# Retention before a feed-forward block: one product of 192 columns for a piece's outputs and its new state

## The chip, the cores and the metric

The kernel runs on one core of a Trainium2 chip. The metric is the device time of one execution in microseconds, a median of several; differences of 0.2% and more can be told from no change. The core has a matrix engine (TensorE, PE in the profile; its weight loads stand apart as PEld), a vector engine (VectorE, DVE), a scalar engine (ScalarE, ACT), a general engine (GpSimd, POOL) and a sync engine (SyncE, SP) that issues nearly all transfers. TensorE writes to PSUM, a small memory of banks of 128 partitions x 512 floats[...].

## The reference

All data are fp32. 8 batches, 8 heads, 576 tokens, 64 columns a head; then 4608 tokens of 512 columns through a feed-forward block of 2048.

```python
scores = scale * np.matmul(q, k.transpose(0, 1, 3, 2))
gamma = 1.0 - 2.0 ** (-5.0 - np.arange(H, dtype=np.float32))
Dmat = np.where(rel >= 0, gamma[:, None, None] ** rel[None, :, :], 0.0)
attn = np.matmul(scores * Dmat[None, :, :, :], v)
x = attn.transpose(0, 2, 1, 3).reshape(B * S, H * D)
h = x @ w_in
sp = np.maximum(h, 0.0) + np.log1p(np.exp(-np.abs(h)))
out = (h * erf(sp)) @ w_out
```

The weights come as float64 and are rounded to fp32 in the kernel. Because the decay is a power of the distance, a batch can be worked through in pieces with a state: a piece's output is its own masked scores times values, plus its queries times the sum of keys x values of all earlier pieces, decayed.

## The kernel before

**Pieces.** A batch of 576 tokens is four pieces of 128 and a rest of 64; the rests of two batches make one piece. That is 36 pieces, numbered from 0 here and in the code; 8, 17, 26 and 35 are the short ones, and 0, 4, 9, 13, 18, 22, 27 and 31 begin a batch and have no earlier state. Each piece has three stages. `transposes` (L315) brings queries and keys into columns: for early pieces on TensorE with ScalarE copying out, later from squares of 32x32 loaded by DMA and turned by VectorE (`STREAM_TRANSPOSE`, L326). `scores` (L341) makes eight products, two heads at a time on the two halves of the array's rows, and VectorE masks them into `sT`. `outputs` (L354) makes, in this order on TensorE,

- eight products values x scores (L365), 128 rows, 64 columns of the array, 128 columns streamed;
- where there is an earlier state, eight products state x queries (L376), 64 rows and 64 columns of the array each;
- for a piece of 128 tokens, eight products values/keys (L388), 64 columns streamed, giving keys x values of this piece (`kv`).

Heads come in four pairs p of two, e; the output of head e of pair p goes to the half (e + p) % 2 of the partitions, so the state products of two pairs lie on four different quarters of the array. Then VectorE scales the outputs into `x` (`scaled`, L400), adds `kv` to the earlier state (L421) and GpSimd multiplies by the decay of 128 tokens (L427; VectorE where the batch begins). The result, `kept[b]`, is the state that the next piece's L376 reads.

**Order.** The stages stand in one list (L434-439): transposes of i + 1, outputs of i, scores of i + 1, and so on. `attend` runs the next of them between two products of the feed-forward block, so on TensorE a stage is followed by a group of eight matrix records ("product") of that block, which is worked in chunks of 512 tokens with a Strassen-like scheme of seven products (`First` for w_in, `Second` for w_out). ScalarE copies the accumulators out (t<-a, o<-a), takes softplus and erf with a table load each; all engines work through their instructions in the order of the program. GpSimd weighs values by the decay (`weigh_values`, L306) before they are used and does part of the weights' rounding.

**Loads.** Rows of keys and values of piece i + 3 are asked for at the end of `outputs(i)` (L430), queries and squares of piece i + 2 in `transposes(i)` (L339), all on SyncE's queue. Rows of keys have four buffers of their own. At the start, `keep_busy` (L735) multiplies a tile of ones while nothing has landed.

Of the kernel before, what the change touches and what calls it, by code (L numbers as in the profile page):

```python
# [18 lines left out]
P = 128  # L19
B, H, S, D = 8, 8, 576, 64  # L20
D_MODEL, D_FF = 512, 2048
NP = H // 2
# [9 lines left out]
def decays():  # L32

    gamma = 1.0 - 2.0 ** (-5.0 - np.arange(H, dtype=np.float64))
    pairs = gamma.reshape(2, NP)
    row = pairs.repeat(D, axis=0)
    out = np.where(np.arange(NP) % 2 == 0, row, np.roll(row, D, axis=0))  # L40
    t = np.arange(P)
    parts = []
    for n in (P, D):
        j = t % n
        i = np.arange(n).reshape(-1, n // 32).T.reshape(-1)
        gk = pairs.T.reshape(1, H) ** -j[:, None]
        gq = out[:, :, None] ** i[None, None, :] / math.sqrt(D)
        i_all = np.concatenate([i + a for a in range(0, P, n)])
        tri = (i_all[None, :] >= t[:, None]) & (i_all[None, :] // n == t[:, None] // n)
        parts += [gk, gq, row**P, tri] if n == P else [gk, gq, tri]  # L50
    return np.concatenate([x.reshape(P, -1) for x in parts], axis=1).astype(np.float32)
# [3 lines left out]
def kernel(  # L55
# [66 lines left out]

    def load_squares(i, name, src):
# [12 lines left out]
    def load_rows(i, name, src, bufs):  # L136
        if name == "q":
            t = raw.tile([P, NP, P * D // SQ], FP32, tag="qs", name="raw_q", bufs=bufs)
            t = t.rearrange("p a x -> p (a x)")[:, : H * D].rearrange("p (h d) -> p h d", h=H)
        else:  # L140
# [23 lines left out]
    ones = cpool.tile([P, P], FP32, name="ones")  # L164
    nc.vector.memset(ones, 1.0)
# [26 lines left out]
    def parts():  # L192

        w2 = w_in.rearrange("(e c d) (h f) -> c e d h f", c=n_dc, d=D, h=2)
        for g in range(n_g):
            for dc in range(n_dc):
                a = A11 if dc < 2 else A12
                src = [(heads[(e + dc) % 2], w2[dc, e, :, :, 2 * g * GW : 2 * (g + 1) * GW]) for e in range(2)]
# [104 lines left out]
    kept = {}  # L303
    weighed = set()

# [9 lines left out]
    def transposes(i):  # L315
        t = live[i] = loaded.pop(i)
        if i < SQUARES:
            weigh_values(i)
# [22 lines left out]
    def scores(i):  # L341
        t = live[i]
        sT = t["sT"] = att.tile([P, 2, NP, P], FP32, tag="sT", name="sT")
# [10 lines left out]
    def outputs(i):  # L354
        segments = pieces[i]
        t = live.pop(i)
# [3 lines left out]

        b, s0, n, _ = segments[0]
        o = [ps_at.tile([P, NP, P], FP32, tag="at", name=f"o{j}") for j in range(2)]
        for p in range(NP):
            for e in range(2):
                nc.tensor.matmul(  # L365
                    o[p % 2][heads[(e + p) % 2], p // 2, :],
                    lhsT=t["v"][:, 2 * p + e, :],
                    rhs=t["sT"][:, e, p, :],
# [4 lines left out]
        for state, r0, m in seen:  # L373
            for p in range(NP):
                for e in range(2):
                    nc.tensor.matmul(  # L376
                        o[p % 2][heads[(e + p) % 2], p // 2, r0 : r0 + m],
                        lhsT=state[heads[e], p, :],
                        rhs=t["qT"][heads[e], p, r0 : r0 + m],
# [4 lines left out]
        if n == P:  # L384
            kv = flat(o[0])[:, 2 * P :].rearrange("p (a d) -> p a d", a=NP)
# [14 lines left out]
        def scaled(j):  # L400
            to = x[0, c][:, j:NP:2, at : at + P]
            if c < n_ch - 1:
                by = (gq if n == P else gq2)[:, j::2, :].unsqueeze(2).to_broadcast([P, 2, P // n, n])
                dst, got = (y.rearrange("p a (m i) -> p a m i", i=n) for y in (to, o[j][:, :2]))
# [3 lines left out]
            for r0 in range(0, P, n):  # L408
# [3 lines left out]
                    for y in (o[j][:, :2, r0 : r0 + n], (gq if n == P else gq2)[:, j::2, :])  # L412
# [4 lines left out]
        if n == P:  # L417
            sums = kv
            if s0 > 0:
                sums = att.tile([P, NP, D], FP32, tag="sums", name="sums")  # L420
                tt(sums, kv, kept[b], ALU.add)  # L421

            if b % 2 == 0 and s0 + P + D == S:
                new = att.tile([P, NP, D], FP32, tag="last", name="last", bufs=1)
            else:
                new = att.tile([P, NP, D], FP32, tag="state", name="state")
# [3 lines left out]
        load(i + 3, "kv")  # L430
# [304 lines left out]
    def keep_busy(n):  # L735
        for _ in range(n):
            nc.tensor.matmul(idle[:, :P], lhsT=ones, rhs=ones, start=True, stop=True)
# [126 lines left out]
```

## Time and profile before

| | |
|---|---|
| time, median of 3 | 1027.68 us (1027.46 to 1027.72) |
| span of the profiled execution | 1024.0 us |
| TensorE busy | 1017.6 us, 99% |
| VectorE, ScalarE, GpSimd busy | 667.6, 390.2, 122.6 us |
| records of L365, L376, L388 | 576, 512, 512; 41.1, 19.5, 21.5 us busy |
| pieces run until | some 314 us |

A fp32 product stands as two records in the profile. Busy time of a group on TensorE is the union of overlapping records, so what a group costs is better read from starts: the start of the next group minus its own. "128*64 128x64" is rows*columns of the array, then partitions x elements streamed. In a group line the figures behind the bar are busy time and mean duration; what stands after the second bar is idle time of the engine just before and what ended it. In the list in order of time the first column is the start, the second the length, and a bracket gives idle time before and what ended it.

### The profile page before, as it was taken

The numbers are of one execution on the slowest core, as the hardware profiler recorded it, in microseconds if no ns is written. First come the engines' busy times: TensorE is split into PE (matmuls) and PEld (weight loads), VectorE is DVE, ScalarE is ACT, GpSimd is POOL, SyncE is SP. The second block draws the span as 40 slices with busy tenths as digits, with TensorE's granted clock in tenths as the row PEclk, the third lists the DMA queues.
The fourth block names the chain that finished last, engine by engine and source line by source line (L and its number), as shares of the span: only waits on it lengthen the run. The fifth ranks groups of instructions, "written<-read, shape, count | busy, mean of one in ns | idle before, by whom it ended". The sixth has DMA issues, their size and how long they took to land.

```text
span 1024.0 us, 15958 instructions
## 1 busy us (share of the span) xinstructions
PE 1017.6 (99%) x6348; PEld 876.0 (86%) x6348; DVE 667.6 (65%) x1062; ACT 390.2 (38%) x481; POOL 122.6 (12%) x122
## 2 busy tenths in 40 slices
PE   9999999999999999999999999999999999999998
PEld 8787888888888888888888888888888888888887
DVE  3769777976976656656666666666567655555555
ACT  3354134234134444334343444444433333333332
POOL 2143112122312110010001001000100000000000
PEclk9999999999999999999999999999999999999999
DMA  9998989979974354544444345444433333444434
GB/s 200 203 242 175 232 203 223 255 150 253 244 195 150 106 161 145 165 160 154 164 147 158 124 147 162 165 144 144 144 124 124 124 131 127 131 136 131 126 88 119
DMA packets 146986, 165.76 MB, mean 162 GB/s; under 512 B 97376, under 2 KB 121568, under 8 KB 138848
## 3 DMA queue, kind: packets, MB, share of 16 engines
q1 hardware_dynamic: 144832, 163.57, 56.4%
q10 hardware_dynamic: 2080, 1.18, 0.5%
q8 instruction: 50, 0.82, 0.4%
q14 instruction: 24, 0.20, 0.1%
HBM read 117.52 MB, written 47.19 MB: 161 GB/s over the span
## 4 chain that ended last, share of the span: by engine, by line
PE 94%; DMA 3%; DVE 2%; SPq 1%; POOL 1%; issue 0%; ACTq 0%; DVEq 0%; POOLq 0%
PE a L604 24%; PE a L496 23%; PE g L604 12%; PE g L496 12%; PE e L496 6%; PE e L604 6%; PE o L365 3%; PE s L347 3%; PE o L388 2%; DMA raw_k<-in_k_dram 1%; PE o L376 1%; DMA raw_v<-in_v_dram 1%; PE f L668 1%; SPq L147 1%; PE p L550 1%; PE h L668 1%
## 5 line engine op out<-in xcount | busy, mean ns | idle before, releaser
L496 PE MATMUL a<-x,wa 128*128 128x256 f32 x1088 | 258.3, 380 | 0.0
L496 PEld LDWEIGHTS a<-x,wa 128*128 128x128 f32 x1088 | 205.7, 190 | 28.5
L604 PE MATMUL a<-wb,s 128*128 128x256 f32 x840 | 200.0, 381 | 0.0
L604 PEld LDWEIGHTS a<-wb,s 128*128 128x128 f32 x840 | 158.4, 190 | 22.9 <-ACT o L618 0.7
L99 DVE TENSOR_TENSOR t<-g,t 128x512 f32<-128x512 f32 x68 | 47.0, 691 | 151.9 <-ACT t L526 114.1
L496 PE MATMUL g<-x,wa 128*128 128x256 f32 x544 | 129.2, 380 | 0.0
L496 PEld LDWEIGHTS g<-x,wa 128*128 128x128 f32 x544 | 102.8, 190 | 14.4
L99 DVE TENSOR_TENSOR o<-a,o 128x512 f32<-128x512 f32 x104 | 71.4, 687 | 46.4 <-PE a L604 46.4
L521 ACT COPY t<-a 128x512 f32<-128x512 f32 x34 | 19.9, 586 | 188.3 <-PE a L496 188.3
L99 DVE TENSOR_TENSOR t<-t,s 128x1024 f32<-128x1024 f32 x72 | 88.4, 1267 | 0.0
L274 POOL TENSOR_TENSOR wraw<-wraw 128x512 f32<-128x512 f32 x28 | 29.4, 1051 | 438.1 <-DVE wraw L272 184.4
L565 ACT ACTIVATE s<-t 128x1024 f32<-128x1024 f32 x72 | 72.1, 1049 | 24.6 <-DVE t L99 24.5
L99 DVE TENSOR_TENSOR x<-x 128x512 f32<-128x512 f32 x115 | 75.8, 693 | 1.2
L532 ACT COPY t<-a 128x512 f32<-128x512 f32 x34 | 19.9, 586 | 144.4 <-PE a L496 144.4
L569 ACT ACTIVATE s<-s 128x1024 f32<-128x1024 f32 x72 | 72.1, 1049 | 0.4
L604 PE MATMUL g<-wb,s 128*128 128x256 f32 x280 | 66.7, 381 | 0.0
L604 PE MATMUL e<-wb,t 128*128 128x256 f32 x280 | 66.6, 380 | 0.0
L604 PE MATMUL a<-wb,t 128*128 128x256 f32 x280 | 66.6, 380 | 0.0
L604 PE MATMUL g<-wb,t 128*128 128x256 f32 x280 | 66.4, 380 | 0.0
L99 DVE TENSOR_TENSOR sT<-s,cst 128x512 f32<-128x512 f32 x72 | 46.2, 682 | 30.4 <-PE s L347 30.4
L496 PE MATMUL e<-x,wa 128*128 128x256 f32 x272 | 64.8, 381 | 0.0
L99 DVE TENSOR_TENSOR o<-g,o 128x512 f32<-128x512 f32 x70 | 47.9, 684 | 20.9 <-ACT o L618 18.1
(86 smaller groups left out, 1247.1 us busy)
## 6 DMA issues: line engine op xcount, KB each, us to landing
od<-o SPq DMA_DIRECT2D x54, 512.0 KB, 3.3
x<-xd SPq DMA_DIRECT2D x27, 1024.0 KB, 4.8
o<-od SPq DMA_DIRECT2D x27, 1024.0 KB, 5.4
raw_qs<-in_q_dram SPq DMA_DIRECT2D x96, 112.0 KB, 4.4
raw_ks<-in_k_dram SPq DMA_DIRECT2D x84, 112.0 KB, 4.2
xd<-x SPq DMA_DIRECT2D x9, 1024.0 KB, 5.2
raw_v<-in_v_dram SPq DMA_DIRECT2D x64, 128.0 KB, 4.5
wraw<-in_moe_w_in_dram SPq DMA_DIRECT2D x32, 256.0 KB, 5.7
```

The lines of the kernel that those rows point to most:

```text
L99: nc.vector.tensor_tensor(out=out, in0=in0, in1=in1, op=op)
L274: engine.tensor_tensor(out=r_f, in0=high_f, in1=r_f, op=ALU.mult)
L347: nc.tensor.matmul(ps[e][:, p, :], lhsT=t["kT"][heads[e], p, :], rhs=t["qT"][heads[e], p, :], start=True, stop=True)
L365: nc.tensor.matmul(o[p % 2][heads[(e + p) % 2], p // 2, :], lhsT=t["v"][:, 2 * p + e, :], rhs=t["sT"][:, e, p, :], start=(p < 2), stop=(no ...
L388: nc.tensor.matmul(kv[heads[e], p, :], lhsT=t["k"][:, 2 * p + e, :], rhs=t["v"][:, 2 * p + e, :], start=False, stop=(p == NP - 1), skip_gr ...
L496: nc.tensor.matmul(acc[:, j * TH : (j + 1) * TH], lhsT=weights["wa", self.g][:, a, d, j * P : (j + 1) * P], rhs=x[self.g, self.c][a][:, d, :],
L521: nc.scalar.copy(out=self.t1[:, 1], in_=self.a)
L532: nc.scalar.copy(out=self.t2[:, 0], in_=self.a)
L565: nc.scalar.activation(self.s[:, j], t, AF.Softplus)
L569: nc.scalar.activation(self.s[:, j], self.s[:, j], AF.Erf)
L604: nc.tensor.matmul(acc[:, tp, :], lhsT=left[:, j * TH + tp * P : j * TH + (tp + 1) * P], rhs=weights["wb", self.g][:, b, j, :], start=(sta ...
L668: nc.tensor.matmul(acc, lhsT=left[:, j * TH + tp * P : j * TH + (tp + 1) * P], rhs=weights["wb", self.g][:, b, j, :], start=(b in (B11, B2 ...
```

## The change

From piece 13 on, the rows of keys stand right beside a head's masked scores in one tile, 128 + 64 columns a head. Values x [scores | keys] is then one product of 192 columns: it gives the outputs and, in the last 64 columns, (keys x values) transposed. VectorE turns that in blocks of 32x32 (`STREAM_TRANSPOSE`), GpSimd adds the earlier state and multiplies by the decay, once into `new` (kept in the turned-block form for the next sum) and once into `whole`, a tile of 128x128 for a pair with one head's 64x64 state in each diagonal quarter and zeros elsewhere. ScalarE then moves the off-diagonal blocks of 32 to their places (`place_state`, four copies), called at the start of the next `transposes` or `outputs` stage. The state product for a piece of 128 tokens becomes four products with the full array. For this each head's output must lie in the half e of the partitions for every pair, in all pieces. Keys' rows, `sT` of early pieces and the new combined slots (three) share one tile `keys`; from piece 13 on rows of keys are loaded two pieces ahead in place of three. `whole`, zero at first, also takes the place of the ones in `keep_busy`.

```diff
--- before.py
+++ after.py
@@ -37,14 +37,13 @@
     gamma = 1.0 - 2.0 ** (-5.0 - np.arange(H, dtype=np.float64))
     pairs = gamma.reshape(2, NP)
     row = pairs.repeat(D, axis=0)
-    out = np.where(np.arange(NP) % 2 == 0, row, np.roll(row, D, axis=0))
     t = np.arange(P)
     parts = []
     for n in (P, D):
         j = t % n
         i = np.arange(n).reshape(-1, n // 32).T.reshape(-1)
         gk = pairs.T.reshape(1, H) ** -j[:, None]
-        gq = out[:, :, None] ** i[None, None, :] / math.sqrt(D)
+        gq = row[:, :, None] ** i[None, None, :] / math.sqrt(D)
         i_all = np.concatenate([i + a for a in range(0, P, n)])
         tri = (i_all[None, :] >= t[:, None]) & (i_all[None, :] // n == t[:, None] // n)
         parts += [gk, gq, row**P, tri] if n == P else [gk, gq, tri]
@@ -120,6 +119,29 @@
     SQUARES_K = 3 * PC
     SQ = 32
 
+    BESIDE = 13
+    WIDE = P + D
+
+    keys = att.tile([P, 3, H * WIDE], FP32, name="keys", bufs=1)
+
+    def beside(i):
+
+        return keys[:, i % 3, :].rearrange("p (h x) -> p h x", h=H)
+
+    def rows_of_keys(i):
+        if i < BESIDE:
+            at = i % 4 * H * D
+            return keys.rearrange("p a x -> p (a x)")[:, at : at + H * D].rearrange("p (h d) -> p h d", h=H)
+        return beside(i)[:, :, P:]
+
+    def scores_of(i):
+        if i < BESIDE:
+            at = (4 * D + i % 2 * P) * H
+            return keys.rearrange("p a x -> p (a x)")[:, at : at + H * P].rearrange(
+                "p (e a j) -> p e a j", e=2, a=NP
+            )
+        return beside(i)[:, :, :P].rearrange("p (a e) j -> p e a j", e=2)
+
     def load_squares(i, name, src):
         t = raw.tile([P, NP, P * D // SQ], FP32, tag=name + "s", name=f"raw_{name}s", bufs=2)
         for b, s0, n, r0 in pieces[i]:
@@ -137,6 +159,8 @@
         if name == "q":
             t = raw.tile([P, NP, P * D // SQ], FP32, tag="qs", name="raw_q", bufs=bufs)
             t = t.rearrange("p a x -> p (a x)")[:, : H * D].rearrange("p (h d) -> p h d", h=H)
+        elif name == "k":
+            t = rows_of_keys(i)
         else:
             t = raw.tile([P, H, D], FP32, tag=name, name=f"raw_{name}", bufs=bufs)
         for b, s0, n, r0 in pieces[i]:
@@ -161,8 +185,9 @@
                 elif name == "v" or i < SQUARES_K or len(pieces[i]) == 1:
                     t[name] = load_rows(i, name, src, 4)
 
-    ones = cpool.tile([P, P], FP32, name="ones")
-    nc.vector.memset(ones, 1.0)
+
+    whole = cpool.tile([P, NP, P], FP32, name="whole")
+    nc.vector.memset(whole, 0.0)
     load(0)
     cst = cpool.tile([P, CONST_COLS], FP32, name="cst")
     nc.sync.dma_start(out=cst[:, :CONST_FIRST], in_=consts[:, :CONST_FIRST])
@@ -195,7 +220,7 @@
         for g in range(n_g):
             for dc in range(n_dc):
                 a = A11 if dc < 2 else A12
-                src = [(heads[(e + dc) % 2], w2[dc, e, :, :, 2 * g * GW : 2 * (g + 1) * GW]) for e in range(2)]
+                src = [(heads[e], w2[dc, e, :, :, 2 * g * GW : 2 * (g + 1) * GW]) for e in range(2)]
 
                 yield src, "wa", g, a, dc % 2, ["wa"] if g > 0 and dc == n_dc - 1 else []
             for f in range(2):
@@ -301,7 +326,21 @@
         return xpool.tile([P, n_dc + 3, TCH], FP32, tag="x", name="x")
 
     kept = {}
+    squares_kept = [None]
+    unplaced = []
     weighed = set()
+
+    def place_state():
+
+        while unplaced:
+            dst, src = unplaced.pop()
+            for e in range(2):
+                for a in range(2):
+                    rows, to = (slice(e * D + x * SQ, e * D + (x + 1) * SQ) for x in (a, 1 - a))
+                    cols = (e * D if dst is whole else 0) + a * SQ
+                    nc.scalar.copy(
+                        out=dst[to, :, cols : cols + SQ], in_=src[rows, :, (1 - a) * SQ : (2 - a) * SQ]
+                    )
 
     def weigh_values(i):
 
@@ -314,6 +353,7 @@
 
     def transposes(i):
         t = live[i] = loaded.pop(i)
+        place_state()
         if i < SQUARES:
             weigh_values(i)
         for name in "qk":
@@ -340,7 +380,7 @@
 
     def scores(i):
         t = live[i]
-        sT = t["sT"] = att.tile([P, 2, NP, P], FP32, tag="sT", name="sT")
+        sT = t["sT"] = scores_of(i)
         ps = [ps_at.tile([P, NP, P], FP32, tag="at", name=f"s{e}") for e in range(2)]
         for p in range(NP):
             for e in range(2):
@@ -353,36 +393,45 @@
 
     def outputs(i):
         segments = pieces[i]
+        place_state()
         t = live.pop(i)
         seen = [(kept[b], r0, n) for b, s0, n, r0 in segments if s0 > 0]
 
 
-
         b, s0, n, _ = segments[0]
+        wide = n == P and i >= BESIDE
         o = [ps_at.tile([P, NP, P], FP32, tag="at", name=f"o{j}") for j in range(2)]
+        kv = flat(o[0])[:, 2 * P :].rearrange("p (a d) -> p a d", a=NP)
+        o = [flat(y).rearrange("p (a x) -> p a x", a=2) if wide else y[:, :2] for y in o]
         for p in range(NP):
             for e in range(2):
+                h = 2 * p + e
                 nc.tensor.matmul(
-                    o[p % 2][heads[(e + p) % 2], p // 2, :],
-                    lhsT=t["v"][:, 2 * p + e, :],
-                    rhs=t["sT"][:, e, p, :],
+                    o[p % 2][heads[e], p // 2, : WIDE if wide else P],
+                    lhsT=t["v"][:, h, :],
+                    rhs=beside(i)[:, h, :] if wide else t["sT"][:, e, p, :],
                     start=(p < 2),
                     stop=(not seen and p >= NP - 2),
                     skip_group_check=True,
                 )
         for state, r0, m in seen:
             for p in range(NP):
+                dst, by = o[p % 2][:, p // 2, r0 : r0 + m], t["qT"][:, p, r0 : r0 + m]
+                if state is whole and n == P:
+                    nc.tensor.matmul(
+                        dst, lhsT=whole[:, p, :], rhs=by, start=False, stop=(p >= NP - 2), skip_group_check=True
+                    )
+                    continue
                 for e in range(2):
                     nc.tensor.matmul(
-                        o[p % 2][heads[(e + p) % 2], p // 2, r0 : r0 + m],
-                        lhsT=state[heads[e], p, :],
-                        rhs=t["qT"][heads[e], p, r0 : r0 + m],
+                        dst[heads[e]],
+                        lhsT=state[heads[e], p, heads[e] if state is whole else slice(0, D)],
+                        rhs=by[heads[e]],
                         start=False,
                         stop=(p >= NP - 2),
                         skip_group_check=True,
                     )
-        if n == P:
-            kv = flat(o[0])[:, 2 * P :].rearrange("p (a d) -> p a d", a=NP)
+        if n == P and not wide:
             for p in range(NP):
                 for e in range(2):
                     nc.tensor.matmul(
@@ -401,7 +450,7 @@
             to = x[0, c][:, j:NP:2, at : at + P]
             if c < n_ch - 1:
                 by = (gq if n == P else gq2)[:, j::2, :].unsqueeze(2).to_broadcast([P, 2, P // n, n])
-                dst, got = (y.rearrange("p a (m i) -> p a m i", i=n) for y in (to, o[j][:, :2]))
+                dst, got = (y.rearrange("p a (m i) -> p a m i", i=n) for y in (to, o[j][:, :, :P]))
                 tt(dst, got, by, ALU.mult)
                 return
 
@@ -409,25 +458,46 @@
                 dst = to[:, :, r0 : r0 + n].rearrange("p h (r a) -> p h a r", r=SQ)
                 got, by = (
                     y.rearrange("p h (a r) -> p h a r", r=SQ)
-                    for y in (o[j][:, :2, r0 : r0 + n], (gq if n == P else gq2)[:, j::2, :])
+                    for y in (o[j][:, :, r0 : r0 + n], (gq if n == P else gq2)[:, j::2, :])
                 )
                 tt(dst, got, by, ALU.mult)
 
         scaled(1)
-        if n == P:
+        last = b % 2 == 0 and s0 + P + D == S
+        if wide:
+
+            sums = att.tile([P, NP, D], FP32, tag="sums", name="sums", bufs=1)
+            for j in (1, 0):
+                nc.vector.transpose(out=sums[:, j::2, :], in_=o[j][:, :, P:WIDE])
+            new = att.tile([P, NP, D], FP32, tag="state", name="state", bufs=1)
+            if s0 > 0:
+                nc.gpsimd.tensor_tensor(out=sums, in0=sums, in1=squares_kept[0], op=ALU.add)
+            nc.gpsimd.tensor_tensor(out=new, in0=sums, in1=gp, op=ALU.mult)
+            squares_kept[0] = new
+            if last:
+                kept[b] = att.tile([P, NP, D], FP32, tag="last", name="last", bufs=1)
+                places = [(slice(0, P), kept[b])]
+            else:
+                kept[b] = whole
+                places = [(heads[e], whole[heads[e], :, heads[e]]) for e in range(2)]
+            for rows, dst in places:
+                nc.gpsimd.tensor_tensor(out=dst, in0=sums[rows], in1=gp[rows], op=ALU.mult)
+            unplaced.append((kept[b], new))
+        elif n == P:
             sums = kv
             if s0 > 0:
-                sums = att.tile([P, NP, D], FP32, tag="sums", name="sums")
+                sums = att.tile([P, NP, D], FP32, tag="sums", name="sums", bufs=1)
                 tt(sums, kv, kept[b], ALU.add)
-
-            if b % 2 == 0 and s0 + P + D == S:
-                new = att.tile([P, NP, D], FP32, tag="last", name="last", bufs=1)
-            else:
-                new = att.tile([P, NP, D], FP32, tag="state", name="state")
+            tag = "last" if last else "state"
+            new = att.tile([P, NP, D], FP32, tag=tag, name=tag, bufs=1)
             (nc.gpsimd if s0 > 0 else nc.vector).tensor_tensor(out=new, in0=sums, in1=gp, op=ALU.mult)
             kept[b] = new
         scaled(0)
-        load(i + 3, "kv")
+        load(i + 3, "kv" if i + 3 < BESIDE else "v")
+
+        for j in range(i + 1 if i + 1 == BESIDE else i + 2, i + 3):
+            if BESIDE <= j < len(pieces) and i + 1 >= BESIDE and len(pieces[j]) == 1:
+                load_rows(j, "k", k, None)
         if i + 1 >= SQUARES:
             weigh_values(i + 1)
 
@@ -734,7 +804,7 @@
 
     def keep_busy(n):
         for _ in range(n):
-            nc.tensor.matmul(idle[:, :P], lhsT=ones, rhs=ones, start=True, stop=True)
+            nc.tensor.matmul(idle[:, :P], lhsT=whole[:, 0], rhs=whole[:, 0], start=True, stop=True)
 
 
     most = [before_chunk(2)]
```

## The prediction

> **What bounds the kernel now.** I read the page's busy times and its chain first, then the sums over the stretch in which the pieces run, then TensorE in order of time around one piece, and last the queues that the change loads.
>
> ```profile
> PE 1017.6 (99%) x6348; PEld 876.0 (86%) x6348; DVE 667.6 (65%) x1062; ACT 390.2 (38%) x481; POOL 122.6 (12%) x122
> ...
> PE 94%; DMA 3%; DVE 2%; SPq 1%; POOL 1%; issue 0%; ACTq 0%; DVEq 0%; POOLq 0%
> ```
>
> TensorE is 94% of the chain. No other engine's saving can show: only less work on TensorE, or fewer waits in the first 90 us, makes the kernel faster. The sum over the stretch from the 12th piece to the last:
>
> ```profile
> 100.00:312.00 212.00, 212.00 (x2013) 172.70 (x2012) 167.31 (x279) 64.62 (x85) 47.58 (x49) 1.00 0.92 221
> ```
>
> The columns are length, PE, PEld, DVE, ACT, POOL, clock, DMA share and GB/s. TensorE never stops here, at full clock. DVE is at 167.31/212 = 79%, DMA at 0.92: both have less room than the whole-span shares say. TensorE in order of time:
>
> ```profile
> 114.08 1.09 PE L365 MATMUL o<-sT,raw_v 128*64 128x128 f32 x16
> 115.00 0.63 PE L388 MATMUL o<-raw_v,raw_k 128*64 128x64 f32 x16
> 115.56 1.99 PE L496 MATMUL a<-x,wa 128*128 128x256 f32 x8
> ...
> 122.23 1.09 PE L365 MATMUL o<-sT,raw_v 128*64 128x128 f32 x16
> 123.26 0.67 PE L376 MATMUL o<-qT,state 64*64 64x128 f32 x16
> 123.85 0.69 PE L388 MATMUL o<-raw_v,raw_k 128*64 128x64 f32 x16
> 124.47 1.99 PE L496 MATMUL a<-x,wa 128*128 128x256 f32 x8
> 126.39 1.16 PE L347 MATMUL s<-qT,kT 64*128 64x128 f32 x16
> ```
>
> Starts are what to subtract. A piece with a state costs 123.26-122.23 = 1.03, then 0.59, then 0.62: 2.24 us. One without costs 0.92 + 0.56. An fp32 product stands as two records, so "x16" is eight products. In the first group 16 records go in pairs (two halves of the columns at once): 8 slots in about 0.92, 109 ns a slot of 128 columns, the rest being the change of tile shape. The state group has 16 records of 64*64 in about the time of 4 slots: heads are placed at (e + p) % 2, so four quarters of the array work at once. This is the packing that the change gives up.
>
> **What the Trainium skill says.** TensorEngine Tiling (Array Packing), Key Properties: changing the tiling mode drains TensorE. The trace agrees: the product after the outputs takes 126.39-124.47 = 1.92 us, against 118.58 to 120.41, 1.83, for one with a change of shape on one side only. TensorE: Matmul & The Clock Gate, LDWEIGHTS: a load takes columns/1.2 ns whatever the rows, an estimate of 107 ns for 128 columns, so a full-array product of 128 columns can't be faster than its load. The trace agrees:
>
> ```profile
> 44.36 0.60 PE L332 MATMUL pt_k<-ident,raw_k 128*128 128x128 f32 x4
> 44.79 1.03 PE L550 MATMUL p<-x,wa 128*128 128x256 f32 x4
> ```
>
> Four full-array records of 128 columns take 44.79-44.36 = 0.43 us, 109 ns each. The same page, Architectural detail: ScalarE and VectorE are strict FIFO, so a copy placed in ScalarE's queue waits for all ahead of it. SBUF — State Buffer, the section on two separate sides: VectorE with two SBUF inputs and GpSimd exclude each other for a whole instruction. The trace fits: four x<-x sums of VectorE at 99.48 take 3.53 us with a GpSimd product of 1.49 us beside them, and 2.59 us at 258.73 without.
>
> **The change part by part, TensorE first.**
> *Wide piece with a state (15 of them: pieces 14-16, 19-21, 23-25, 28-30, 32-34, counted from 0).* Removed: the state group 0.59 and the key group 0.62. The output group streams 192 in place of 128 columns: 8 slots x 64/128 x 107 ns = +0.43, so 1.45. The state becomes four 128x128 products, 8 records that can't be packed: 8 x 109 ns = 0.87, plus 0.10 for the exposed first load, 0.97. Then the array is already in full shape, so the next product is 1.83 in place of 1.92. After: 1.45 + 0.97 + 1.83 = 4.25; before: 2.24 + 1.92 = 4.16. +0.09 x 15 = +1.4 us.
> *Wide piece without a state (5).* 0.92 + 0.56 = 1.48 becomes 0.92 + 0.43 + 0.09 = 1.44: -0.04 x 5 = -0.2 us. So one product of 192 columns saves loads and shape changes, but not columns.
> *Narrow pieces.* heads[e] in place of heads[(e + p) % 2] puts all four pairs on the same two quarters: two at a time, not four. The state group goes from 4 to 8 slots, +0.44 us. Nine pieces have it (1-3, 5-7, 10-12). The first three lie in the start, whose chain is DMA and its issue: hidden. Six remain: +2.6 us (none of 5-7, if the stretch to 87 us hides them: +1.3). The four short pieces (8, 17, 26, 35) go from 0.62 to 1.09: +0.47 each; the first lies where the chain is on VectorE, so three: +1.4 us.
>
> **Waits that it adds.**
> *Keys of piece 13.* Rows of keys are now asked for at the outputs two pieces ahead, for 13 one piece ahead, behind the values of 15, since the slot holds data of piece 12 until its outputs are done.
>
> ```profile
> 107.46 2.77 SPq L131 DMA_DIRECT2D raw_ks<-in_k_dram  x4
> 110.33 0.38 SPq L709 DMA_DIRECT2D od<-o  x1
> 110.80 1.38 SPq L147 DMA_DIRECT2D raw_k<-in_k_dram  x2
> 112.28 1.16 SPq L147 DMA_DIRECT2D raw_v<-in_v_dram  x2
> ```
>
> In the changed order values take the place at 110.80 and these keys the one at 112.28. The second transfer is issued near 112.9 and lands 4.4 us later (median of such rows), at 117.3. The product that needs it stood at 114.08 and moves by 0.44 against this queue: a wait of +2.8 us on TensorE, once (1 to 4).
> *The turned state.* After the outputs: VectorE's first scaling (0.33 apart in a row), two transposes of 128 columns (not in the trace; 128x256 took 0.42 and 128x512 0.70, so 0.28 each, at most 0.42), GpSimd's sum and three products of 256 elements (0.61 each by the state row, 0.57 apart: 2.3), then four ScalarE copies of 128 elements on 32 partitions (not in the trace; 128x512 takes 0.58 from PSUM, 0.68 from SBUF; SBUF forms of 1024 and 512 stand 0.96 and 0.57 apart, so 0.27 apart: 1.2 to 1.6 with the waits). Together some 4.9 us where sums and state took 1.1. The next state product comes 6.66 + 1.45 = 8.1 us after the outputs' end, so with VectorE up to 1.6 us late and GpSimd's value product behind it, it fits. What decides is ScalarE's order. The copies are issued with the transposes of the piece after next, mostly behind an o<-a or t<-a copy that ends 1.1 us before the outputs begin; placing ends 0.3 us into them, 1.1 before the need. One place differs, piece 14:
>
> ```profile
> 127.10 1.28 ACT L565 ACT_TABLE_LOAD   x1
> 130.24 2.00 ACT L565 ACTIVATE s<-t 128x1024 f32<-128x1024 f32 x2 [1.86 <-DVE t L99]
> 132.15 0.56 ACT L618 COPY o<-a 128x512 f32<-128x512 f32 x1
> ```
>
> Its copies stand right behind the two softplus, which wait for VectorE: placing runs from 132.2 to 133.5, and the state product is due at 131.13 + 1.45 = 132.6: +0.9 us. The o<-a copy behind is 1.3 later, but its bank is next written at 136.39: nothing. For the last piece only 4.9 us lie between outputs, and GpSimd's three added products push its value product past the need: +0.3.
> *Contention.* 20 x 2.3 us of GpSimd replace 15 x 0.6; some VectorE sums are held. VectorE keeps some 0.8 us of lead in the transposes before the scores: I take +0.6 in all (0 to 3).
> Hidden: 80 ScalarE copies (24 us on an engine with 147 idle there), the larger memset at the start, the bytes (equal).
>
> Sum: 1.4 - 0.2 + 2.6 + 1.4 + 2.8 + 0.9 + 0.3 + 0.6 = +9.8, 1027.7 + 9.8 = **1037.5 us**.
>
> **The rivals.**
> *Only the columns count*: keys land in time and ScalarE is never late. 1.4 - 0.2 + 2.6 + 1.4 = +5.2: 1033. For it: the landing is a median, and the queue carries two transfers fewer just before. Against: the order of that queue.
> *The state comes late everywhere*: copies at 0.45 us and VectorE held by GpSimd eat the 1.1 us of lead; 15 pieces x 1.2 us more: 1055. For it: four engines in a row at 79% VectorE. Against: 8.1 us for 4.9 of work.
> *Faster*: shape changes cost more than I read and the two that go save 0.3 us a piece, while the start hides the narrow pieces: 20 x -0.3 + 2.8 = -3.2: 1024.5. For it: two changes of shape fewer per piece. Against: the starts already contain them.
> *No change*, all losses hidden in the start: 1028.
>
> **How the numbers follow.** Forecast 0.58, only columns 0.20, late state 0.12, faster 0.06, no change 0.04. The range holds the first two and the bounds of keys, placing and contention: 1031 to 1044. Slower by over 0.2% is 0.58 + 0.20 + 0.12 = 0.90.
>
> **What would show it.** In the changed profile the wide group takes 1.45 us from start to start, the full state group 0.97, narrow state groups 1.0 instead of 0.59. TensorE shows a wait for the keys' DMA near 115 us and one for a ScalarE copy near 133, and few others. The products outside stay at 380 ns. I am wrong if the narrow state groups still take 0.6, if the wide group costs less than 1.3, or if TensorE waits for ScalarE in most pieces.

## The result and the profile after

| | before | after |
|---|---|---|
| time, median (lowest to highest) | 1027.57 us (1027.05 to 1027.72) | 1040.82 us (1039.84 to 1041.57) |
| ratio | | 1.0129 (95%: 1.0112 to 1.0147) |
| span of the profiled execution | 1024.0 us | 1038.9 us |

The change makes the kernel slower by 1.3%, about 13.3 us. The profiled execution is 14.9 us longer, and that is the sum to be explained below. The profiled execution of the kernel before took 1025.83 us, 1.7 us below its median, which is why the spans differ by 1.6 us more than the medians; where it saved them is not known. First the busy times of the page of after, and the line of shares in its chain:

```profile
PE 1026.7 (99%) x5908; PEld 883.2 (85%) x5908; DVE 680.1 (65%) x1082; ACT 414.3 (40%) x561; POOL 168.1 (16%) x180
...
PE 84%; issue 4%; POOL 3%; SPq 3%; DVE 2%; DMA 2%; ACT 1%; DVEq 0%; POOLq 0%; ACTq 0%
```

TensorE has 440 records fewer and is busy for 9.1 us more. Its share of the chain falls from 94% to 84%: other engines now end some of its waits. Which ones, its list of waits in the profile of after tells (total, times, longest):

```profile
PE o L409 <- DMA keys<-in_k_dram: 2.2, 1, 2.2
PE o L409 <- POOL raw_v L352: 1.8, 4, 0.7
PE idle L807 <- DVE whole L190: 1.4, 1, 1.4
PE o L421 <- ACT whole L341: 0.9, 1, 0.9
```

The third is the larger tile that is set to zero at the very start, when nothing has landed yet. The others lie where pieces run. The sum over the same stretch as before:

```profile
100.00:312.00 212.00, 208.32 (x1525) 168.68 (x1522) 167.17 (x280) 84.02 (x154) 84.83 (x97) 0.99 0.90 209
```

TensorE is short of 3.7 us, the clock is 0.99 in place of 1.00, GpSimd has 84.83 in place of 47.58. Now TensorE in order of time, from the narrow piece 12 to the first wide piece, 13. Before:

```profile
106.20 0.67 PE L376 MATMUL o<-qT,state 64*64 64x128 f32 x16
106.80 0.69 PE L388 MATMUL o<-raw_v,raw_k 128*64 128x64 f32 x16
107.41 1.99 PE L604 MATMUL g<-wb,t 128*128 128x256 f32 x8
...
131.13 1.09 PE L365 MATMUL o<-sT,raw_v 128*64 128x128 f32 x16
```

After:

```profile
109.69 1.08 PE L426 MATMUL o<-qT,state 64*64 64x128 f32 x15
110.70 0.69 PE L437 MATMUL o<-raw_v,keys 128*64 128x64 f32 x16
111.31 1.99 PE L674 MATMUL g<-wb,t 128*128 128x256 f32 x8
...
116.16 1.89 PE L566 MATMUL g<-x,wa 128*128 128x256 f32 x8
120.21 3.32 PE L409 MATMUL o<-keys,raw_v 128*64 128x192 f32 x16 [2.16 <-DMA keys<-in_k_dram]
123.46 2.24 PE L566 MATMUL a<-x,wa 128*128 128x256 f32 x8
```

The narrow state group takes 110.70-109.69 = 1.01 us where the kernel before needs 106.80-106.20 = 0.60. The product at 111.31 started at 107.41 before: 3.9 us are lost by then. Then TensorE waits 2.16 us for the keys of piece 13, and the wide group takes 123.46-120.21 = 3.25 us, against 1.45 in nearly all others. Why, the sums by stretch show (columns as in the sum above; the clock is the third figure from the end):

```profile
118.00:120.20 2.20, 0.05 (x1) 0.02 (x1) 0.00 (x0) 0.00 (x0) 0.00 (x0) 1.00 1.10 252
121.00:122.00 1.00, 1.00 (x8) 0.82 (x7) 0.00 (x0) 0.00 (x0) 0.00 (x0) 0.50 0.86 237
...
124.00:125.00 1.00, 1.00 (x6) 0.88 (x5) 0.72 (x3) 0.00 (x0) 0.42 (x1) 1.00 1.05 233
```

The clock falls to one half soon after the idle stretch and stays there for some 3 us. The prediction had the wait and not this.

A later wide piece, 14, with the placing that the prediction was afraid of, from the list in order of time:

```profile
130.37 1.52 PE L409 MATMUL o<-keys,raw_v 128*64 128x192 f32 x16
131.82 1.16 PE L421 MATMUL o<-qT,whole 128*128 128x128 f32 x8
132.81 1.89 PE L566 MATMUL a<-x,wa 128*128 128x256 f32 x8
...
138.48 2.00 ACT L635 ACTIVATE s<-t 128x1024 f32<-128x1024 f32 x2 [1.86 <-DVE t L98]
139.38 1.52 PE L409 MATMUL o<-keys,raw_v 128*64 128x192 f32 x16
140.51 1.25 ACT L341 COPY whole<-state 32x128 f32<-32x128 f32 x4
...
141.82 1.16 PE L421 MATMUL o<-qT,whole 128*128 128x128 f32 x8 [0.92 <-ACT whole L341]
```

The wide group is 131.82-130.37 = 1.45 us, the full state group 0.99. From one wide group to the next are 139.38-130.37 = 9.01 us, where the kernel before has 131.13-122.23 = 8.90. ScalarE's four copies stand behind softplus and end 0.92 us too late, at this one place. Elsewhere ScalarE's copies end in time.

### The profile page after: what moved, and what is told of

Same layout as the page of the kernel before. It is cut to its first block, busy times and chain, and to the rows that moved or that the text cites. A ratio compares the mean times of both kernels' runs of the same rounds, so it can differ in the third digit from the quotient of the medians.

```text
span 1038.9 us, 15275 instructions
## 1 busy us (share of the span) xinstructions
PE 1026.7 (99%) x5908; PEld 883.2 (85%) x5908; DVE 680.1 (65%) x1082; ACT 414.3 (40%) x561; POOL 168.1 (16%) x180
## 4 chain that ended last, share of the span: by engine, by line
PE 84%; issue 4%; POOL 3%; SPq 3%; DVE 2%; DMA 2%; ACT 1%; DVEq 0%; POOLq 0%; ACTq 0%
PE a L566 21%; PE a L674 21%; PE g L566 11%; PE g L674 11%; PE e L674 5%; PE e L566 5%; PE o L409 3%; PE s L387 2%; SPq L171 1%; POOL raw_v L352 1%; SPq L153 1%; DMA keys<-in_k_dram 1%; POOL whole L484 1%; PE o L421 1%; PE o L426 1%
## 5 line engine op out<-in xcount | busy, mean ns | idle before, releaser
L98 DVE TENSOR_TENSOR keys<-s,cst 128x512 f32<-128x512 f32 x72 | 46.2, 682 | 26.8 <-PE s L387 26.8
## 6 DMA issues: line engine op xcount, KB each, us to landing
x<-xd SPq DMA_DIRECT2D x27, 1024.0 KB, 4.8
o<-od SPq DMA_DIRECT2D x27, 1024.0 KB, 5.2
xd<-x SPq DMA_DIRECT2D x9, 1024.0 KB, 5.1
```

The costliest lines, as they stand in the source:

```text
L98: nc.vector.tensor_tensor(out=out, in0=in0, in1=in1, op=op)
```

## The experiments

Every time below is compared with the kernel before on the same chip, whose medians were 1026.8, 1027.3 and 1027.2 us in the three groups of runs; a ratio of 1.0100 is 10.3 us. Differences in microseconds are worked out from the ratio, which lies up to 0.0008 from the quotient of the medians; its interval (95%, in brackets) reaches some 0.0013 to either side. So times alone do not separate two of these kernels by less than some 1.5 us, and smaller steps are read from the traces.

**The placement alone.** The kernel before, with this and nothing else of the change (the decays' rows and the rows of w_in follow):

```diff
-                    o[p % 2][heads[(e + p) % 2], p // 2, :],
+                    o[p % 2][heads[e], p // 2, :],
...
-                        o[p % 2][heads[(e + p) % 2], p // 2, r0 : r0 + m],
+                        o[p % 2][heads[e], p // 2, r0 : r0 + m],
```

> The kernel before with one thing of the change alone: every pair's head e goes to half e of the partitions, in the products, the decay table and the order of the weights' rows. No wide product, no turned state. Theory (four quarters of the array at once are lost): the state group goes from 0.60 to 1.02 us in 24 pieces and from 0.62 to 1.07 in 4, 24 x 0.43 + 4 x 0.46 = 12.2, less some 0.6 hidden in the first 40 us: about 1039. Rival (the narrow pieces' loss in the changed kernel came from waits, not from the packing): 1028, state group still 0.6.

Measured: 1036.59 us, ratio 1.0093 (1.0079 to 1.0107), some 9.6 us. TensorE in order of time in this kernel, piece 12:

```profile
109.11 1.09 PE L376 MATMUL o<-qT,state 64*64 64x128 f32 x16
110.14 0.69 PE L388 MATMUL o<-raw_v,raw_k 128*64 128x64 f32 x16
```

1.03 us in place of 0.60, and no new wait: the loss of packing is real, and no other part of the change that was tried apart costs as much. (It counts in all 28 pieces with a state here; the changed kernel has 13 such groups left.) It costs less than counted out, 2 us less by the ratio and 0.7 by the profiled spans (1034.9 and 1024.0). By 41 us this kernel is 0.8 us behind, no more than kernels below that keep the packing (0.3 to 1.2): the narrow groups of pieces 1 to 3, some 1.3 us, are hidden as far as these profiles show, where the working had 0.6.

**Keys early.** The changed kernel with the combined slots in another turn, so that the slot of piece 13 holds no data of piece 12 and keys are asked for two pieces ahead from the start:

```diff
-        return keys[:, i % 3, :].rearrange("p (h x) -> p h x", h=H)
+        return keys[:, (i + 1) % 3, :].rearrange("p (h x) -> p h x", h=H)
...
-        for j in range(i + 1 if i + 1 == BESIDE else i + 2, i + 3):
-            if BESIDE <= j < len(pieces) and i + 1 >= BESIDE and len(pieces[j]) == 1:
-                load_rows(j, "k", k, None)
+        if BESIDE <= i + 2 < len(pieces) and len(pieces[i + 2]) == 1:
+            load_rows(i + 2, "k", k, None)
```

> The changed kernel with the three combined slots used in another order, so that piece 13 lies where nothing of piece 12 stands and its keys can be asked for two pieces ahead like all others. Theory (one late transfer costs 2.2 us of waiting and, because TensorE then ran at half its clock until 124, another 2.0): both go, about 4.2 us less than the changed kernel, 1036.6, mean clock 1.00. Rival A (only the wait goes, the slow clock has another cause): 2.2 less, 1038.6. Rival B (the wait moves to values or to the squares, since the queue is as full as before): less than 1 us.

Measured: 1036.53 us, 1.0088 (1.0074 to 1.0102), so some 4 us less than the changed kernel. The wait is gone, the wide group of piece 13 takes 1.45 us, the clock is 1.0. Wait and slow clock together cost 4 us; that the clock follows from the wait is tried below.

**Values first.** GpSimd weights the next piece's values ahead of its work for the state:

```diff
+        if i + 1 >= SQUARES:
+            weigh_values(i + 1)
         if wide:
...
-        if i + 1 >= SQUARES:
-            weigh_values(i + 1)
```

> The changed kernel with GpSimd's product of the next piece's values put ahead of the sum and products of the state, not behind. Theory (TensorE's waits of 0.1 to 0.75 us before pieces 17, 26, 30, 34 and 35 come from the four GpSimd products of the state standing before the values): they go, 2.2 us less, 1038.6; the state comes 1.1 us later and may cost up to 1 us of it. Rival (VectorE's exclusion of GpSimd is what delays the values, wherever they stand): no less than 0.5 us, waits stay.

Measured: 1036.99 us, 1.0097 (1.0084 to 1.0111). The waits for weighted values are gone, with two new ones of 0.3 us for queries and keys. The gain is larger than expected for a reason that is not the edit's: the wait for keys was 1.9 us here, the clock stayed at 1.0, and the wide group of piece 13 took 1.98 us, not 3.25. (The 0.5 us over 1.45 are a second wait inside the group, as its keys come in two transfers.)

**Place first.** The state is placed ahead of softplus as well, in the step that leads to it:

```diff
             tt(self.t1[:, 1], self.e, self.t1[:, 1], ALU.add)
+            place_state()
             self.softplus()
```

> The changed kernel with ScalarE's four placing copies also called right before the two softplus of a chunk. Theory (the state product of piece 15 waits 0.9 us because the copies stand behind two softplus that wait for VectorE): that wait goes, 1.0 us less, 1039.8. Rival (the state isn't ready on GpSimd by then, so the copies hold softplus and what follows): no gain or slower by up to 1 us.

Measured: 1038.87 us, 1.0114 (1.01 to 1.0127); the wait for ScalarE is gone. In this profile, too, the keys' wait was 1.9 us without a slow clock, and the mean clock was 0.998 in two of the four runs and 0.999 or 1.0 in the others; so the 0.9 us can't be read from the total alone. It can from the wait.

**TensorE kept busy while it waits.** The keys come as late as in the changed kernel, but eleven products of zeros, which nobody reads, stand ahead of the wide group of piece 13:

```diff
+        if i == BESIDE:
+            for _ in range(11):
+                nc.tensor.matmul(o[0][:, 0, :P], lhsT=whole[:, 0], rhs=whole[:, 0], start=True, stop=True)
```

> The changed kernel with eleven 128x128 products of zeros on TensorE right before the wide product of piece 13, 22 records x 109 ns = 2.4 us, so that TensorE works while those keys land; all results are the same. Theory (the keys' wait costs twice, once as waiting and once as a clock at half speed after it, when it passes about 2 us): no wait shown, clock 1.00, wide group of piece 13 at 1.45 us; 1.8 to 2.0 us less than a run with the slow clock, and about 0.4 more than one whose wait stays under 2 us. Rival (the wide group is slow for another reason, such as its operands still arriving): the group still takes over 3 us.

Measured: 1038.83 us, 1.011 (1.0095 to 1.0126). TensorE in order of time, and one of the sums by stretch, all of which have clock 1.00:

```profile
117.74 2.62 PE L408 MATMUL o<-whole 128*128 128x128 f32 x22
120.29 1.58 PE L412 MATMUL o<-keys,raw_v 128*64 128x192 f32 x16
121.80 1.99 PE L569 MATMUL a<-x,wa 128*128 128x256 f32 x8
```

```profile
121.00:122.00 1.00, 1.00 (x12) 0.72 (x9) 0.10 (x1) 0.00 (x0) 0.00 (x0) 1.00 0.96 295
```

The wide group starts as late as in the changed kernel (120.29 and 120.21), but takes 121.80-120.29 = 1.51 us in place of 3.25. The slow clock came from TensorE standing still, not from the keys or from the wide product's form. In the total the gain is 1.1 us against one measurement of the changed kernel and 1.9 against the other, so it is shown by the trace rather than by the time.

**Two mends together**, keys early and place first.

> The changed kernel with both mends: piece 13's keys two pieces ahead, and placing before the softplus. Theory (the two are separate): 2 to 4 us less for keys and 1.3 for placing, so about +8.3 over the kernel before, 1035; left are the lost packing and GpSimd's values. Rival (one mend moves its wait onto the other): no better than the keys' mend alone, +9.7.

Measured: 1034.75 us, 1.0076 (1.0063 to 1.0089). As expected.

**All three mends.**

> The changed kernel with all three mends: keys two pieces ahead from the start, the state placed ahead of softplus, and the next piece's values weighted on GpSimd ahead of its work for the state. The two mends of keys and place left 7.5 to 7.9 us over the kernel before, of which 1.8 us are TensorE's waits for weighted values. Theory (those waits are work of TensorE's path): 5.5 to 6.5 us over, about 1033. Rival (GpSimd's order only moves the wait to the state, as when values alone were put first and new waits of 0.3 us for queries and keys appeared): 7.5 us over, 1035. In both, what then remains is the narrow part before piece 13 (3.9 us, the first 13 pieces at half the quarters) and 0.1 us a wide piece.

Measured: 1033.60 us, 1.0056 (1.0043 to 1.007), 5.8 us over the kernel before, in the theory's band. The waits for values are gone, but at pieces 23 and 25 there are new ones, for keys and for turned keys:

```profile
205.27 1.80 PE L409 MATMUL o<-keys,raw_v 128*64 128x192 f32 x16 [0.59 <-DMA keys<-in_k_dram]
...
226.40 1.49 PE L409 MATMUL o<-keys,raw_v 128*64 128x192 f32 x14 [0.42 <-DVE kT L366]
```

From the output group of piece 26 to that of piece 35 this kernel loses 2.0 us less than the one with two mends: so much was the late values' share of TensorE's path. But from piece 22 to 26 it loses 2.0 us more, and the profiled span is only 0.7 us shorter (1032.0 and 1032.7). The rival's idea, that the wait moves, is thus right for much of it in this execution. The ratios show the full 2 us, but the intervals of 1.0056 and 1.0076 overlap, so the net gain is not settled. What is left after the three mends is mostly the packing.

**Packed again.** Can the wide product be had without giving up the packing? VectorE turns the odd pairs into the other half of the partitions, the state stays 64 columns wide, and outputs and state products go to four quarters again:

```diff
-                    o[p % 2][heads[e], p // 2, : WIDE if wide else P],
+                    o[p % 2][heads[(e + p) % 2], p // 2, : WIDE if wide else P],
...
-            for j in (1, 0):
-                nc.vector.transpose(out=sums[:, j::2, :], in_=o[j][:, :, P:WIDE])
+            for e in range(2):
+                nc.vector.transpose(out=sums[heads[e], 1::2, :], in_=o[1][heads[1 - e], :, P:WIDE])
+            nc.vector.transpose(out=sums[:, ::2, :], in_=o[0][:, :, P:WIDE])
```

> The changed kernel with heads at half (e + p) % 2 again and the state in 64 columns, used in quarters as in the kernel before; VectorE turns the odd pairs' blocks into the other half of the partitions (one transpose more), and GpSimd writes the state once in place of twice. The wide product and the late keys stay. Theory (packing lost is most of the loss): wide piece with a state 1.45 + 0.60, 0.2 us less than before; narrow and short pieces as before. Left are the keys' 2 to 4 us and up to 1 us of placing: 1027.5 - 3 + 4 = about 1028.5. Rival (the turned state's path is the loss): 1035 or more.

Measured: 1037.98 us, 1.0105 (1.0091 to 1.0119). The expectation missed by 9.5 us. On TensorE the groups are as worked out, but the waits took the gain:

```profile
PE o L410 <- POOL raw_v L353: 3.1, 4, 2.0
PE o L410 <- DMA keys<-in_k_dram: 2.5, 1, 2.5
...
PE o L410 <- DMA raw_qs<-in_q_dram: 1.0, 1, 1.0
```

**Packed, with two mends** (keys early, place first).

> The packed form with both mends, keys two pieces ahead and placing before softplus. Theory: the wide product is worth 15 x 0.2 us and nothing waits: 3 us less than the kernel before, 1024. Rival (GpSimd's longer chain still delays the values of pieces 17 to 35): 1025 to 1027, waits for raw_v in the profile.

Measured: 1035.22 us, 1.0077 (1.0065 to 1.009). Missed again, by 11 us:

```profile
PE o L410 <- POOL raw_v L353: 4.2, 5, 2.0
PE o L410 <- DMA keys<-in_k_dram: 4.2, 4, 1.8
```

Up to 151 us this kernel is only 1.0 us behind the kernel before; all the rest is lost at waits behind that. The keys were asked for two pieces ahead and still came late.

**Packed, with three mends.**

> Narrow products spread over all four quarters again, with the three mends. The packed version with two mends was 7.9 us over the kernel before, with 4.2 us of waits for GpSimd's weighted values, 4.2 us for keys that came late though asked for two pieces ahead, and some 1 us for queries. Theory (two separate waits): values first takes the 4.2 us for values, and 3.5 to 5 us over the kernel before are left, about 1031, with the keys' waits still there. Rival (a shared bound, the transfers: with one wait gone TensorE arrives earlier, and waits for keys instead): 7 to 8 us over, as before.

Measured: 1034.24 us, 1.006 (1.0048 to 1.0073), 6.2 us over: nearer to the rival. Values no longer make TensorE wait, but keys still do, and new waits appear (turned queries 1.1 us, turned keys 0.6, and 1.0 at the last piece, which the profile puts down to GpSimd's state). The longest one stands here, in the list in order of time:

```profile
209.50 4.37 SPq L154 DMA_DIRECT2D raw_qs<-in_q_dram  x8
213.97 4.75 SPq L154 DMA_DIRECT2D raw_ks<-in_k_dram  x8
218.83 2.59 SPq L172 DMA_DIRECT2D raw_v<-in_v_dram  x4
221.46 1.16 SPq L172 DMA_DIRECT2D keys<-in_k_dram  x2
...
224.43 0.83 PE L410 MATMUL o<-keys,raw_v 128*64 128x192 f32 x2 [2.13 <-DMA keys<-in_k_dram]
225.54 2.64 PE L410 MATMUL o<-keys,raw_v 128*64 128x192 f32 x14 [0.28 <-DMA keys<-in_k_dram]
```

A short piece follows, and its squares are sixteen transfers (eight of queries, eight of keys) where others have eight, and its values four in place of two. The keys for 224.43 stand behind them in SyncE's queue. They go out from 221.46 on, 0.8 us before TensorE is ready for them (224.43-2.13 = 222.30), and the first land 3 us after that issue. And the clock falls to half again, from 224.5 to 227.9: the 14 records that were left took 2.57 us.

**Packed, keys three ahead.** From piece 16 on, keys are asked for as soon as the piece that has their slot is done:

```diff
-        if BESIDE <= i + 2 < len(pieces) and len(pieces[i + 2]) == 1:
-            load_rows(i + 2, "k", k, None)
+        for j in range(i + 2 if i <= BESIDE else i + 3, i + 4 if i >= BESIDE else i + 3):
+            if BESIDE <= j < len(pieces) and len(pieces[j]) == 1:
+                load_rows(j, "k", k, None)
```

> As the run before, with the keys of every piece from the 16th on asked for three pieces ahead and not two, as soon as the piece that has their slot is done. Theory (the keys were late since their issue stood behind the squares' transfers of a queue that goes in order): the waits for keys go as well, and 0 to 2 us over the kernel before are left, 1027 to 1029. Rival (the transfers' rate sets it, so an earlier place in the queue for keys makes queries or values late): 4 us over or more, with waits for queries or values in place of those for keys. Neither expects to be over 1 us faster than the kernel before, since the packed change gives TensorE the same two products less, 0.2 us a wide piece for 15 pieces, and the start's narrow pieces nothing.

Measured: 1029.56 us (22 runs), 1.0023 (1.0017 to 1.003), 2.4 us over the kernel before. The same place in this kernel, in order of time:

```profile
208.33 1.00 SPq L172 DMA_DIRECT2D keys<-in_k_dram  x2
209.42 4.35 SPq L154 DMA_DIRECT2D raw_qs<-in_q_dram  x8
213.87 4.44 SPq L154 DMA_DIRECT2D raw_ks<-in_k_dram  x8
```

The keys go out ahead of the sixteen, 13 us earlier, and the wide groups no longer wait for keys. The theory of the queue's order holds, though the total is 0.4 us above its band: other waits took part of the gain.

```profile
PE s L388 <- DVE kT L367: 2.0, 3, 1.2
...
PE o L410 <- POOL state L474: 1.0, 1, 1.0
```

The second wait stands at the last piece. Its product reads no state, and VectorE was masking the scores that it does read from 314.68 on, 0.8 us before the product begins at 315.46; so what ended this wait is open.

```profile
123.01 1.52 PE L410 MATMUL o<-keys,raw_v 128*64 128x192 f32 x16
...
131.72 1.52 PE L410 MATMUL o<-keys,raw_v 128*64 128x192 f32 x16
```

From wide group to wide group this kernel takes 131.72-123.01 = 8.71 us against 8.90 before: 0.19 us a piece. An estimate for 15 pieces, 2.9 us, is what the one product of 192 columns is worth on TensorE. The waits, and 0.8 us of the start, take more than it gives. No version tried beats the kernel before.

**The changed kernel again**, beside the last three.

> The changed kernel once more, beside the three versions it is compared with. Every theory: a ratio near 1.013, 13 to 14 us over the kernel before, with the wait of about 2 us for the keys of piece 13; if the wait is below 2 us in the profile, the slow clock behind it may be absent, and the profiled span 2 us shorter.

Measured: 1040.44 us, 1.0121 (1.0103 to 1.0139). The wait for keys was 2.65 us and the wide group of piece 13 took 3.15:

```profile
119.00:120.00 1.00, 0.00 (x0) 0.00 (x0) 0.00 (x0) 0.00 (x0) 0.00 (x0) 0.83 1.07 264
120.00:121.00 1.00, 0.92 (x5) 0.70 (x7) 0.00 (x0) 0.00 (x0) 0.00 (x0) 0.50 1.04 351
...
123.00:124.00 1.00, 1.00 (x6) 0.69 (x5) 0.66 (x3) 0.00 (x0) 0.00 (x0) 0.97 1.13 238
```

A mean of 0.83 is a fall at 119.66, one of 0.97 a return at 123.06: half clock for 3.4 us, from 2.2 us after the last product's end at 117.44.

## Why the prediction was right

1037.5 us were forecast and 1040.8 measured, inside the range. The mechanism was right: columns on TensorE, not products, set the price, packing is worth more than the changes of shape that go, and of the new waits only a few single ones are seen. That the total fell inside is owed to a range 13 us wide: keys, values and the start each came out 1.3 us or more too small, and nothing made up for it. The profiles have:

| term of the sum | predicted | in the profiles | |
|---|---|---|---|
| wide piece with a state, 15 | +1.4 | +1.6 | 9.01 - 8.90 a piece; wide group 1.45, full state group 0.99 as worked out |
| wide piece without | -0.2 | about -0.1 | piece 13 apart |
| narrow pieces | +2.6 | +2.5 | 1.02 a group as worked out; the loss from 42 to 111 us, short piece 8 in it |
| short pieces, the last three | +1.4 | +1.5 | 1.07 a group |
| keys of piece 13 | +2.8 | +4.2 | 2.2 of wait and 2.0 of slow clock behind it |
| placing of piece 14 | +0.9 | +0.9 | |
| values late, contention | +0.3 + 0.6 | +2.2 | five late output groups, 0.05 to 0.8 each; the list of waits has 1.8 of it |
| start, up to 42 us | 0 | +1.4 | a wait of 0.92 in it; 0.3 to 1.2 in the other runs |
| not foreseen | 0 | +0.3 | wide group of piece 19, 1.79 |
| sum | +9.8 | +14.5 | span: +14.9 |

*The start.* The working took the first three narrow pieces as hidden, and they were. At the outputs of piece 5, near 41 us, the changed kernel is 1.35 us behind in one profile and 0.75 in the other, the seven versions without packing 0.4 to 1.2, and the four that keep it, which have no narrow loss at all, 0.3 to 1.2. So these losses are not the narrow groups'; they are measured against a single, fast execution of the kernel before, and their cause is open. From there to 111 us all nine profiles without packing lose 2.5 us, to 0.1 us what the working had.

*The keys.* The wait was read rightly from the queue: issue behind the values of piece 15, landing after the need. The half clock behind it was not in the working. The Trainium skill, TensorE: Matmul & The Clock Gate, the section What's actually happening, says that the array falls to half clock after an idle window of about 3.4 us and returns after a busy one, with windows that run freely. The windows agree: in the traces' record of the clock half speed lasts 3.413 us in all four cases inside the work, and the full-speed stretches before and after are whole multiples of that (33 and 268 in the run above). That the window must be idle does not: the windows that ended in a fall held 2.09 to 2.21 us without a product on TensorE (the changed kernel twice, the packed one, the packed one with three mends), and the emptiest one that did not end so held 1.92 (place first). So it counts where a stop lies. In the packed kernel 2.54 us of stop were followed by the fall 1.4 us after TensorE had started again, while stops of 1.78 and 1.00 us in two windows (packed, two mends) left the clock alone. Since nothing here says where the windows will lie, a stop of over 2 us in a dense stream may cost nearly twice.

*GpSimd.* Its sum and three products for the state take 2.8 us a piece in the mean (0.73, 0.70 and twice 0.68) where the working had 2.3. What was smaller still in the working is what they do to the work behind them. The value product of the last piece but one, from the list in order of time of after:

```profile
315.99 3.19 DVE L98 TENSOR_TENSOR t<-t,s 128x1024 f32<-128x1024 f32 x2
316.07 2.03 POOL L352 TENSOR_TENSOR raw_v<-raw_v,cst 128x512 f32<-128x512 f32 x1
...
318.15 1.59 PE L409 MATMUL o<-keys,raw_v 128*64 128x192 f32 x16 [0.55 <-POOL raw_v L352]
```

The state's chain pushes it into VectorE's long sums with two inputs from SBUF, the memory that holds the tiles. There it takes 2.03 us in place of 1.04, and TensorE waits. The prediction had values past the need for the last piece alone; they came late at five, in four of them with a product of 1.9 to 2.03 us, at the last with one of 1.10. The kernel before has such slow products too (2.02 at 187.08), with nothing waiting for them. Values first takes these waits away.

*The rivals.* Only the columns: columns, packing and shapes alone give +5.5 by the table's first four terms, and the changed kernel with all mends has +5.8 by its ratio; so that rival describes what the changed kernel could be, not what it is. Late state everywhere: refuted, one wait of 0.92 us. Faster: refuted; with packing kept the product does save 0.19 us a piece. No change: refuted as well.

*Where a faster TensorE goes.* In the changed kernel's form the mends led from 1.0121 over 1.0088 and 1.0076 to 1.0056, packed from 1.0105 over 1.0077 and 1.006 to 1.0023. Packing alone was worth 9.6 us in the kernel before, and 2 us in the changed kernel while keys and values were late. The expectations of both packed kernels failed on one mistake: they took the waits of the slower kernel as given, though a TensorE that arrives earlier meets the queue and GpSimd where they were just in time. For the keys the last version shows it. Another cause was not tried apart: the packed form gives VectorE more to turn, 0.94 us a piece where the changed kernel has 0.57.

What stays open: the 2.0 us of waits for turned keys and the 1.0 us at the last piece in the best version, which were not tried apart, the scatter of the start, and why a window that is idle for some 2.1 us is enough to halve the clock.

## What to carry to other kernels

Count a group of products on TensorE by its columns divided by how many of them the array works on at once: merging two products saved little (0.19 us of 8.90 here), and a layout that the merger needs can cost more (0.4 us a group of eight, at every user of it). Before moving a load later or adding work to a helper engine, write down the order of the queue it stands in, look for the piece with more transfers than the others, and reckon that a wait of over 2 us on TensorE may be paid nearly twice. When a mend on the busiest engine gives less than it should, list the waits again: a supplier that was just in time may now be late.

## What the hardware showed that was not expected

- The granted clock changed only at the ends of windows of 3.413 us. With TensorE idle for 2.09 to 2.21 us of a window it fell to half for the next one, and 1.5 to 2 us were lost on top of the wait; with 1.92 us or less it did not fall. Products of zeros during the wait kept it at 1.00.
- Eight products of 64*64 with 128 columns: 0.60 us on the four quarters of the array, 1.02 on two.
- GpSimd's product of 128x512: 1.04 us in most places and 2.03 beside two of VectorE's sums with two SBUF inputs, which then take 3.19 us together (2.6 in the mean).
- Small moves are dear for what they carry: ScalarE's copy of 32x128 takes 0.30 us, four of them 1.25; VectorE's turning of 128x128, 0.29 in the mean.
